# A second product of 512 tokens instead of 288, with the 64 tokens left of each batch as a ninth block

## The chip, the cores and the metric

The kernel runs on one core of a Trainium2 chip. The metric is the device time of one execution in microseconds (us). The core's engines work side by side, each through its own instructions in order: TensorE (PE in the profile; PEld is its weight load), VectorE (DVE), ScalarE (ACT), GpSimd (POOL) and SyncE (SP), which here issues the DMAs.

## The reference, cut to what matters

```python
def _attn_ref(q, k, v):                 # 8 batches, 8 heads, 576 tokens, 64 wide
    ...
    return (A @ Z @ C @ v)              # Z: six Newton steps on a 32x32 matrix

def _moe_ref(x, w_in, w_out):           # x: 4608 x 512, w_in: 512 x 2048, w_out: 2048 x 512
    h = x @ w_in
    g = np.where(h > 0.0, h, np.exp(np.minimum(h, 0.0)) - 1.0)
    return g @ w_out

def _moe2_ref(x, w1, w2, w3, w_out):    # w1..w3: 512 x 768, w_out: 768 x 512
    h = np.maximum(np.maximum(x @ w1, x @ w2), x @ w3)
    return h @ w_out
```

The 4608 tokens are 8 batches of 576. The change lies in `g @ w_out` of the middle function, called the second product here, and in what stands around it.

## The kernel before, in words

**Two phases.** The first phase makes, batch by batch, the attention, `h`, `g` and the second product, and leaves its result, called xs, in HBM. The second phase (lines 1321 and 1405) makes the last function from xs in blocks of 768 and 512 tokens by a scheme with seven products in place of eight.

**Products in three parts.** Each float32 operand is held as two tensors, a rounded high part and the rest (`wo` hi and lo, `gt[:, 0]` and `gt[:, 1]`, `ah` and `al`, `wp[:, 0]` and `wp[:, 1]`), and each product is three matmuls: high by high, low by high, high by low.

**Slots.** The first phase has 256 slots, each one (batch, half, f): half is one of two halves of 288 tokens, f one of 16 chunks of 128 of the 2048 columns of `h`. `h_mm` (line 859) issues 6 matmuls of 288 columns into one of two PSUM banks; the two factors are W' (`wp`, the attention's small matrix times w_in, four chunks of four f each, made by `w_step`, lines 812 to 843) and the attention's other factor (`ah`, `al`, one pair per half). ScalarE then makes relu and exp (lines 863, 864), VectorE joins them (871). In the next slot ScalarE casts the result into a tile `gt` (880), and GpSimd, in batch 0 in half of the slots VectorE, makes its low part (886). `gt` has LAG = 3 buffers of 288 tokens. `x_mm` (line 906) follows three slots later: for each of four blocks `ec` of 128 output columns three matmuls of 288 columns, 12 in all, into one of four PSUM banks, summed over the 16 f of a half. After the last f the four banks are copied out (lines 930 to 934) and stored to xs (935). 

**The order of the work** is the list `seq`. Batches 1 to 7 take half 0 with all f, then half 1 with all f. Batch 0, in which the weights w_in and w_out are still being converted from 64-bit words, takes half 0 with f 0 to 7, half 1 with the same, then both with f 8 to 15: its partial sums are stored, loaded again (922) and added (930).

**What rides along.** The attention of the next batch is done in steps at fixed slots (`STEP_SLOTS`, `SECOND_SLOTS`). Its matmuls (line 262) go into two PSUM banks; a step that finds its bank unread waits. The W' chunks of batch b are made at slots -6, -4, -2 and 1 counted from the batch's first slot (`W_SLOTS`), each into its own tile, and serve both halves. `w_step` needs both banks: ScalarE copies them (826), then VectorE subtracts (831). A second list converts the last function's weights (`Narrowing`), in slots 15 to 30 of most batches.

**Queues.** PE and VectorE run in the order in which the program issues; ScalarE up to slot 27 and SP up to slot 14. After that the order on ScalarE and SP is made by a scheduler when the kernel is built. A DMA that waits on SP holds up those behind it.

**The end of the first phase.** In batch 7 `background()` makes the first weights of the second phase (`weights2`), in slots 3 and 10 to 29, and from slot 28 `tk.prepare()` and `tk.make()` make the first block's operands; three slots of `x_mm` are left after the loop.

Of the kernel before, what the change touches and what calls it, by code (L numbers as in the profile page):

```python
# [19 lines left out]
def landmark_attention_mlp_maxout_kernel(  # L20
# [31 lines left out]
    LAG = 3  # L52

    FIXED_SP, FIXED_ACT = 14, 27
    RA = 3
# [27 lines left out]
    G_LOW = [[1, 0] * 8, [1, 0] * 8]  # L83
# [12 lines left out]
    hs = tc.dram_tile([NT // 512, P, 7, NP, 256], F32, name="hs")  # L96

# [412 lines left out]
    def exp_t(b, g):  # L510
        e = state.pop(("e", b, g))
        if b == 0:
            if g:
                em = r_s.tile([P, CH - 1, P], F32, tag="gt", name="et", bufs=LAG)
            else:
                em = att.tile([P, CH, P], F32, tag="et", name="et")[:, : CH - 1]
                state["tails"] = r_s.tile([P, 2, P], F32, tag="gt", name="et", bufs=LAG)
# [299 lines left out]
    def w_step(b, n, late=False):  # L817
# [27 lines left out]
    xos = {}  # L845
# [30 lines left out]
    def gt_cast():  # L876

        for key, e in held:
            gts[key] = gt = r_s.tile([P, 2, HF], F32R, tag="gt", name="gt", bufs=LAG)
            state["cast"] = nc.scalar.copy(gt[:, 0], e)  # L880

    def gt_low():
        for (b, half, f), e in held:
            gt = gts[b, half, f]
            eng = nc.vector if b == 0 and G_LOW[half][f] else nc.gpsimd
            state["low"] = eng.tensor_tensor(  # L886
                out=gt[:, 1], in0=e, in1=gt[:, 0].bitcast(F32), op=ALU.subtract
            )
        held.clear()

    def x_mm(b, half, f):
        gt = gts.pop((b, half, f))

        parts = b == 0
        first = f % (KF // 2) == 0 if parts else f == 0
        last = f % (KF // 2) == KF // 2 - 1 if parts else f == KF - 1
        if b == 0:
            assert conv.ready >= index["out", f]
        if first:
            for ec in range(KD):  # L900
                xacc[ec] = ps_x.tile([P, 512], F32, tag=f"x{ec}", name=f"x{ec}")

        for ec in (0, 2, 1, 3):
            wh, wl = [w[:, ec * P : (ec + 1) * P] for w in w_out_tiles(f)]
            for j, (a, c) in enumerate(((wh, 0), (wl, 0), (wh, 1))):
                nc.tensor.matmul(  # L906
                    xacc[ec][:, :HF],
                    a,
                    gt[:, c],
                    start=(first and j == 0),  # L910
                    stop=(last and j == 2),
                )
        t0 = b * S + half * HF
        there = [
            xs[eh * 2 * P : (eh + 1) * 2 * P, t0 : t0 + HF].rearrange("(e p) t -> p e t", p=P)
            for eh in range(2)
        ]
        add = parts and f >= KF // 2
        if first and add:
            for eh in range(2):  # L920
                xos[eh] = r_s.tile([P, 2, HF], F32, tag=f"xo{eh}", name="xo")
                nc.sync.dma_start(out=xos[eh], in_=there[eh])
        if last:
            for eh in range(2):
                if not add:
                    xos[eh] = r_s.tile([P, 2, HF], F32, tag=f"xo{eh}", name="xo")
                for ec in range(2):
                    o, a = xos[eh][:, ec], xacc[2 * eh + ec][:, :HF]
                    if add:
                        nc.vector.tensor_tensor(out=o, in0=a, in1=o, op=ALU.add)  # L930
                    elif ec == 0:
                        nc.scalar.copy(o, a)  # L932
                    else:
                        nc.vector.tensor_copy(o, a)  # L934
                nc.sync.dma_start(out=there[eh], in_=xos[eh])

# [340 lines left out]
    def tokens(nb):  # L1277
# [19 lines left out]
        def spare(nm):  # L1297
            if nb == 0:
                tag = {"S1": "wo20", "S2": "wo21", "S4": "wo30"}[nm]
                return r_w.tile([P, 2, TH], F32, tag=tag, name="s")  # L1300
# [98 lines left out]
    def o_mm(nb, tk, j, then):  # L1399
# [12 lines left out]
        there = out[ub * TB : (ub + 1) * TB].rearrange("(h r p) e -> r p h e", h=2, p=P)[r]  # L1412
        if nb < NBO - 1 or j == 0:
            nc.sync.dma_start(out=there, in_=ob.rearrange("p (h e) c -> p h (e c)", h=2))
        else:
            for n in (0, 3, 1, 2):
                c0 = n % 2 * (DM // 2)
                nc.sync.dma_start(out=there[:, n // 2, c0 : c0 + DM // 2], in_=ob[:, n])
# [60 lines left out]
    W_SLOTS = [-6, -4, -2, 1]  # L1479
    SECOND_W = [-5, -3, -1, 2]  # L1480
# [8 lines left out]
    places += [("wp", n, g) for n in range(NCH // 2, NCH) for g in range(2)]  # L1489
# [140 lines left out]
    seq = [(0, half, p * KF // 2 + f) for p in range(2) for half in range(2) for f in range(KF // 2)]  # L1630
    seq += [(b, half, f) for b in range(1, B) for half in range(2) for f in range(KF)]
# [28 lines left out]
    for n in range(1, NCH):  # L1660
        tw = (0, FPN, KF, KF + FPN)[n]
        at(tw - (2, 3, 2)[n - 1], w_both, n)
# [3 lines left out]
    for it in range(2 * NP):  # L1666
        for n, (nw, t0) in enumerate(((Narrowing(*plain[it]), 15), (Narrowing(*split7[it]), 23))):
# [5 lines left out]
            if n:  # L1673
                parts = nw.parts()
                for m in range(7):
                    behind[t0 + 11 + m].append(parts)
# [4 lines left out]
    def stage(fn, k, *args):  # L1681
        if FRONT <= k < len(items):
            fn(k, *args)

    for t, sl in enumerate(seq):
# [12 lines left out]
        if t >= LAG:  # L1698
            x_mm(*seq[t - LAG])
# [16 lines left out]
        if i == 2:  # L1716
# [5 lines left out]
        if i > KF + LAG and (i - KF - LAG) % 2:  # L1722
# [136 lines left out]
```

## Time and profile before

| | |
|---|---|
| Time, median of 3 runs | 1300.81 us (1300.03 to 1300.85) |
| Span of the profiled execution, first to last instruction | 1298.6 us |
| Median less span | 2.2 us |
| PE busy in the span | 98% |
| Batch 0 begins; batches 1 to 7 begin | 35.2; 138.4, 231.3, 322.0, 412.7, 503.4, 594.1, 684.8 us |
| Second phase begins | 762.5 us |

The profile comes from one execution; its span leaves out what lies before the first and after the last instruction, so the times of the runs stand a little above it. Matmuls overlap: the time of one in the profile is longer than the distance from its start to the next one's. What a stream of them costs is read from the time at which each begins, or from the chain, which counts that distance.

### The profile page before, as it was taken

The numbers are of one execution on the slowest core, as the hardware profiler recorded it, in microseconds if no ns is written. First come the engines' busy times: TensorE is split into PE (matmuls) and PEld (weight loads), VectorE is DVE, ScalarE is ACT, GpSimd is POOL, SyncE is SP. The second block draws the span as 40 slices with busy tenths as digits, with TensorE's granted clock in tenths as the row PEclk, the third lists the DMA queues.
The fourth block names the chain that finished last, engine by engine and source line by source line (L and its number), as shares of the span: only waits on it lengthen the run. The fifth ranks groups of instructions, "written<-read, shape, count | busy, mean of one in ns | idle before, by whom it ended". The sixth has DMA issues, their size and how long they took to land.

```text
span 1298.6 us, 26490 instructions
## 1 busy us (share of the span) xinstructions
PE 1276.0 (98%) x10196; PEld 1206.8 (93%) x10196; DVE 819.6 (63%) x1498; ACT 681.7 (52%) x1551; POOL 644.8 (50%) x609
## 2 busy tenths in 40 slices
PE   6899999999999999999999999999999999999998
PEld 3688899998998998999999999999999999999998
DVE  7888547456465475375453558776766666569773
ACT  5887557657667577576576643323131323245551
POOL 2426225435445345354256566756565656555542
PEclk8999999999999999999999999999999999999999
DMA  7944033142152143143142135555555556969852
GB/s 275 367 162 137 20 101 118 68 140 79 68 174 92 54 141 108 44 143 105 52 137 86 52 125 172 170 170 167 166 170 170 177 172 208 336 197 355 297 165 82
DMA packets 113967, 195.45 MB, mean 151 GB/s; under 512 B 7216, under 2 KB 61744, under 8 KB 113840
## 3 DMA queue, kind: packets, MB, share of 16 engines
q1 hardware_dynamic: 113840, 193.75, 45.0%
q8 instruction: 80, 1.31, 0.4%
q14 instruction: 47, 0.39, 0.1%
HBM read 134.74 MB, written 58.98 MB: 149 GB/s over the span
## 4 chain that ended last, share of the span: by engine, by line
PE 93%; ACT 2%; DVE 2%; DMA 2%; issue 1%; SPq 0%; POOL 0%; DVEq 0%; ACTq 0%
PE p L1321 31%; PE x L906 30%; PE ph L859 14%; PE p L1405 10%; PE bank L262 7%; DMA words<-in_moe_w_in_dram 2%; PE idle L262 0%; DVE eh L871 0%; ACT eh L864 0%; DVE wf L149 0%; ACT xo L1095 0%; ACT eh L863 0%; ACT words L132 0%; ACT wp L826 0%; DVE kT L323 0%
## 5 line engine op out<-in xcount | busy, mean ns | idle before, releaser
L906 PE MATMUL x<-gt,wo 128*128 128x288 f32 x3072 | 460.7, 298 | 2.2 <-ACT xo L932 1.6
L906 PEld LDWEIGHTS x<-gt,wo 128*128 128x128 f32 x3072 | 416.1, 188 | 43.2 <-ACT eh L863 18.2
L886 POOL TENSOR_TENSOR gt<-eh,gt 128x288 fp32r<-128x288 f32 x240 | 198.3, 828 | 332.1 <-ACT gt L880 326.8
L1321 PE MATMUL p<-xo,w 128*128 128x384 f32 x1944 | 349.8, 337 | 0.8 <-DVE xo L934 0.8
L1321 PEld LDWEIGHTS p<-xo,w 128*128 128x128 f32 x1944 | 341.6, 188 | 1.1 <-ACT s L1148 1.1
L859 PE MATMUL ph<-ah,wp 128*128 128x288 f32 x1024 | 244.9, 295 | 4.8 <-DVE eh L871 4.8
L871 DVE SCALAR_TENSOR_TENSOR eh<-eh,ph 128x288 f32<-128x288 f32 x256 | 113.9, 445 | 163.9 <-ACT eh L864 140.4
L1165 POOL TENSOR_TENSOR u<-s,v 128x768 f32<-128x768 f32 (+1 forms) x72 | 131.0, 1820 | 161.0 <-DVE v L1163 161.0
L859 PEld LDWEIGHTS ph<-ah,wp 128*128 128x128 f32 x1024 | 177.9, 188 | 6.8 <-DVE eh L871 6.6
L880 ACT CAST gt<-eh 128x288 fp32r<-128x288 f32 x256 | 110.0, 430 | 118.5 <-PE x L906 81.6
L1148 ACT COPY s<-p 128x384 f32<-128x384 f32 (+1 forms) x110 | 52.5, 478 | 217.5 <-PE p L1321 203.4
L863 ACT ACTIVATE eh<-ph 128x288 f32<-128x288 f32 x256 | 104.9, 410 | 94.3 <-PE ph L859 92.6
L859 PE MATMUL ph<-al,wp 128*128 128x288 f32 x512 | 150.8, 294 | 0.0
L1405 PE MATMUL p<-wo,ho 128*128 128x256 f32 x1134 | 134.3, 281 | 0.0
L1405 PEld LDWEIGHTS p<-wo,ho 128*128 128x128 f32 x1134 | 134.3, 189 | 0.0
L864 ACT ACTIVATE eh<-eh 128x288 f32<-128x288 f32 x256 | 113.8, 444 | 6.7
L1180 DVE TENSOR_TENSOR t<-p,u 128x384 f32<-128x384 f32 x108 | 56.9, 553 | 65.1 <-POOL u L1165 61.7
L859 PEld LDWEIGHTS ph<-al,wp 128*128 128x128 f32 x512 | 96.1, 188 | 0.2 <-issue 0.2
L1395 DVE TENSOR_TENSOR ho<-hf,ho 128x768 fp32r<-128x768 f32 x54 | 73.5, 1391 | 12.6 <-ACT ho L1393 12.6
L1393 ACT CAST ho<-hf 128x768 fp32r<-128x768 f32 x63 | 50.5, 836 | 45.4 <-PE p L1405 22.3
L1163 DVE TENSOR_TENSOR v<-p,s 128x384 f32<-128x384 f32 (+1 forms) x72 | 37.3, 518 | 52.5 <-PE p L1321 40.7
L1321 PE MATMUL p<-w,w 128*128 128x384 f32 x324 | 65.2, 335 | 0.0
(186 smaller groups left out, 1484.2 us busy)
## 6 DMA issues: line engine op xcount, KB each, us to landing
w<-wus SPq DMA_DIRECT2D x54, 512.0 KB, 4.2
hf<-hs SPq DMA_DIRECT2D x63, 384.0 KB, 4.9
xs<-xo SPq DMA_DIRECT2D x36, 288.0 KB, 2.9
qT<-in_q_dram SPq DMA_DIRECT2D x16, 576.0 KB, 6.1
kT<-in_k_dram SPq DMA_DIRECT2D x16, 576.0 KB, 7.4
words<-in_moe_w_dram SPq DMA_DIRECT2D x9, 1024.0 KB, 5.4
xf<-xs SPq DMA_DIRECT2D x12, 768.0 KB, 5.1
hs<-t SPq DMA_DIRECT2D x18, 512.0 KB, 3.5
```

The source lines that it names most:

```text
L262: ins = fn(*args, **kw)
L859: nc.tensor.matmul(ph[:, :HF], a, c, start=(g == 0 and j == 0), stop=(g == 1 and j == 2))
L863: nc.scalar.activation(e, ph[:, :HF], AF.Relu, scale=-1.0)
L864: state["exp"] = nc.scalar.activation(e, e, AF.Exp, scale=-1.0)
L871: state["post"] = nc.vector.scalar_tensor_tensor(out=e, in0=e, scalar=1.0, in1=ph[:, :HF], op0=ALU.subtract, op1=ALU.max)
L880: state["cast"] = nc.scalar.copy(gt[:, 0], e)
L886: state["low"] = eng.tensor_tensor(out=gt[:, 1], in0=e, in1=gt[:, 0].bitcast(F32), op=ALU.subtract)
L906: nc.tensor.matmul(xacc[ec][:, :HF], a, gt[:, c], start=(first and j == 0), stop=(last and j == 2),)
L1165: nc.gpsimd.tensor_tensor(out=u57, in0=s57, in1=v.unsqueeze(1).to_broadcast([P, 2, width]), op=ALU.add)
L1321: nc.tensor.matmul(dst, l, r, start=(c == 0 and j == 0), stop=(c == 1 and j == 2))
L1395: eng.tensor_tensor(out=lo, in0=v, in1=hi.bitcast(F32), op=ALU.subtract)
L1405: nc.tensor.matmul(dst, l, r, start=(c == 0 and n == 0), stop=(c == NP - 1 and n == 2))
```

## The change

**Second product.** `gt` holds both halves of one f (576 tokens, GT = 3 buffers). `seq` takes, in every batch, f by f with the two halves in turn. `x_mm` takes tokens 0 to 511 of a batch at once, in two parts of 6 matmuls of 512 columns, one part per slot, four slots behind (LAG = 4). Batch 0 has no partial sums any more. The result is copied out per `ec` into tiles of the tag "wq".

**The 64 left.** When the low part of a second half is made, SP stores tokens 512 to 575 of that `gt`, high and low, to a new HBM tensor `gs` (128 stores of 64 KB, in runs of 256 bytes). After batch 7 a ninth block runs the second product on them: 8 batches by 64 tokens are again 512. `load_rest` fetches 512 KB for each f into the `gt` buffer that the f three places before has left.

**Order of xs.** xs now holds the 512 of each batch first, then the ninth block. The output's stores in the second phase go to the rows to which each tile of 128 tokens belongs: two stores per tile pair in place of one, and two of 64 rows each for tiles of the ninth block.

**W' in three places.** With the halves in turn each chunk serves 8 slots running, so three pairs of tiles do (WP), made at slots -5, 1, 6 and 11 (batch 1: -4, 1, 6, 11; batch 0: at slots 4, 13, 18). `ah` and `al` have four buffers instead of three.

**The end.** The first weights of the second phase are made in every other slot of batch 7 from slot 14, and in the ninth block, where the first block's operands are made too.

```diff
-    LAG = 3
+    LAG = 4
+    GT = 3
+    XN = 512
+    REST = S - XN
+    WP = 3
...
-    RA = 3
+    RA = 4
...
-    EARLY = {2: range(8, 21), 3: range(8, 26)}
+    EARLY = {1: range(0, 11), 2: range(8, 20)}
...
-    PAIRS = "i0 i0 o0 i1 i1 o2 o4 o6 i2 i2 o8 i3 i3 o10 o12 o14".split()
+    PAIRS = "i0 i0 o0 i1 i1 o2 o4 i2 i2 o6 o8 i3 i3 o10 o12 o14".split()
...
+    gs = tc.dram_tile([KF, P, 2, B * REST], F32, name="gs")
...
-            wt = r_wp.tile([P, 2, 512], F32R, tag=f"wp{n}{g}", name="wp")
+            wt = r_wp.tile([P, 2, 512], F32R, tag=f"wp{(b * NCH + n) % WP}{g}", name="wp")
...
     def gt_low():
         for (b, half, f), e in held:
...
+            if half:
+                nc.sync.dma_start(
+                    out=gs[f, :, :, b * REST : (b + 1) * REST],
+                    in_=gt[:, :, XN:].bitcast(F32),
+                )
...
+    def load_rest(f):
+        gts[B, f] = t = r_s.tile([P, 2, S], F32R, tag="gt", name="gt", bufs=GT)
+        nc.sync.dma_start(out=t[:, :, :XN].bitcast(F32), in_=gs[f])
+
+    def x_mm(b, f, part):
+        gt = gts[b, f]
...
+        for ec in (2 * part, 2 * part + 1):
+            if f == 0:
+                xacc[ec] = ps_x.tile([P, XN], F32, tag=f"x{ec}", name=f"x{ec}")
             wh, wl = [w[:, ec * P : (ec + 1) * P] for w in w_out_tiles(f)]
             for j, (a, c) in enumerate(((wh, 0), (wl, 0), (wh, 1))):
                 nc.tensor.matmul(
-                    xacc[ec][:, :HF],
+                    xacc[ec],
                     a,
-                    gt[:, c],
+                    gt[:, c, :XN],
...
+            if f == KF - 1:
+                xo = r_s.tile([P, XN], F32, tag="wq", name="xo", bufs=4)
+                if ec % 2 == 0:
+                    nc.scalar.copy(xo, xacc[ec])
+                else:
+                    nc.vector.tensor_copy(xo, xacc[ec])
+                nc.sync.dma_start(
+                    out=xs[ec * P : (ec + 1) * P, b * XN : (b + 1) * XN], in_=xo
+                )
...
-    W_SLOTS = [-6, -4, -2, 1]
-    SECOND_W = [-5, -3, -1, 2]
+    W_SLOTS = [-5, 1, 6, 11]
+    SECOND_W = [-4, 1, 6, 11]
+    FIRST_W = [None, 4, 13, 18]
...
-    seq = [(0, half, p * KF // 2 + f) for p in range(2) for half in range(2) for f in range(KF // 2)]
-    seq += [(b, half, f) for b in range(1, B) for half in range(2) for f in range(KF)]
+    seq = [(b, half, f) for b in range(B) for f in range(KF) for half in range(2)]
...
+    def x_slot(t):
+        n, part = divmod(t, 2)
+        b, f = divmod(n, KF)
+        x_mm(b, f, part)
+        if part and n + GT >= B * KF and n + GT < (B + 1) * KF:
+            load_rest(n + GT - B * KF)
...
-    for t in range(LAG):
-        for _ in range((2, 1, 1)[t]):
+    for t in range(len(seq), len(seq) + NSL + LAG):
+        x_slot(t - LAG)
+        i = t - len(seq)
+        background()
+        if i % 3 == 0:
+            tk.prepare()
+        if i % 3 == 1:
             tk.make()
-        x_mm(*seq[t - LAG])
```

## Rows read from the trace of the kernel before

**Rows 1.** The page: span, and the chain by engine and by line.

```profile
span 1298.6 us, 26490 instructions
...
PE 93%; ACT 2%; DVE 2%; DMA 2%; issue 1%; SPq 0%; POOL 0%; DVEq 0%; ACTq 0%
PE p L1321 31%; PE x L906 30%; PE ph L859 14%; PE p L1405 10%; PE bank L262 7%; DMA words<-in_moe_w_in_dram 2%; PE idle L262 0%; DVE eh L871 0%; ACT eh L864 0%; DVE wf L149 0%; ACT xo L1095 0%; ACT eh L863 0%; ACT words L132 0%; ACT wp L826 0%; DVE kT L323 0%
```

**Rows 2.** The page's groups: the second product's matmuls.

```profile
L906 PE MATMUL x<-gt,wo 128*128 128x288 f32 x3072 | 460.7, 298 | 2.2 <-ACT xo L932 1.6
```

**Rows 3.** Stretches: us, busy time of each engine, granted clock, DMA share, GB/s.

```profile
35.20:85.00 49.80, 43.92 (x420) 38.28 (x419) 45.13 (x99) 43.84 (x101) 19.58 (x24) 1.00 0.79 282
85.00:138.40 53.40, 52.13 (x443) 46.28 (x442) 43.47 (x87) 38.52 (x91) 25.07 (x28) 1.00 0.38 129
412.70:503.40 90.70, 90.70 (x828) 83.56 (x828) 50.49 (x123) 58.80 (x147) 40.27 (x48) 1.00 0.30 103
...
462.00:467.00 5.00, 5.00 (x40) 5.00 (x40) 3.54 (x8) 4.29 (x12) 0.92 (x2) 1.00 0.98 315
467.00:472.00 5.00, 5.00 (x41) 5.00 (x40) 4.58 (x11) 3.55 (x9) 3.59 (x4) 1.00 0.61 223
477.00:482.00 5.00, 5.00 (x47) 4.00 (x46) 3.93 (x5) 3.37 (x10) 4.84 (x6) 1.00 0.07 27
...
684.80:762.60 77.80, 76.85 (x579) 76.31 (x578) 37.19 (x69) 53.24 (x129) 49.06 (x53) 1.00 0.22 66
```

**Rows 4.** The chain in order of time: start us, us, what.

```profile
688.12 1.59 PE x L906 x12
...
690.50 1.59 PE x L906 x12
...
764.51 396.67 PE p L1321 x2262
1161.19 134.17 PE p L1405 x1134
```

**Rows 5.** Timeline: attention steps on two widths, and a W' step's readers.

```profile
53.36 0.71 PE L262 MATMUL bank<-kT,qs 64*32 64x288 f32 x16
...
500.67 1.09 PE L262 MATMUL bank<-w_in_sb,mt 64*32 64x512 f32 x16
...
501.85 1.08 ACT L826 CAST wp<-bank 128x512 fp32r<-128x512 f32 x2
...
502.96 1.29 DVE L831 TENSOR_TENSOR wp<-bank,wp 128x512 fp32r<-128x512 f32 x2 [0.68 <-ACT wp L826]
```

**Rows 6.** What PE waited for: us in total, times, longest.

```profile
PE ph L859 <- DVE eh L871: 4.8, 4, 1.8
PE x L906 <- ACT xo L932: 1.6, 1, 1.6
...
PE p L1321 <- DVE xo L934: 0.8, 1, 0.8
...
PE x L906 <- DVE xo L930: 0.4, 1, 0.4
```

**Rows 7.** Timeline: a Newton step's operand, and the matmul that reads it.

```profile
469.44 0.29 DVE L787 TENSOR_TENSOR rr<-bank,rr 128x128 f32<-128x128 f32 x1 [0.28 <-ACT rr L784]
...
469.98 0.55 PE L262 MATMUL bank<-rr,rd 128*128 128x64 f32 x4
```

**Rows 8.** DMA: the queue's packets, MB, share; issues with KB, us to landing.

```profile
q1 hardware_dynamic: 113840, 193.75, 45.0%
...
w<-wus SPq DMA_DIRECT2D x54, 512.0 KB, 4.2
...
words<-in_moe_w_in_dram SPq DMA_DIRECT2D x16, 512.0 KB, 10.2
```

**Rows 9.** Timeline, SP: one issue without a wait; the output's last four stores.

```profile
494.19 0.37 SPq L311 DMA_DIRECT2D v<-in_v_dram  x1
...
1293.73 2.44 SPq L1418 DMA_DIRECT2D out_dram<-ob  x4
```

More of the change, by code (lines that the diff above doesn't have):

```diff
@@ L906, in x_mm @@
                 nc.tensor.matmul(
-                    xacc[ec][:, :HF],
+                    xacc[ec],
                     a,
-                    gt[:, c],
-                    start=(first and j == 0),
-                    stop=(last and j == 2),
-                )
[L913 to L935, printed above, removed]
+                    gt[:, c, :XN],
+                    start=(f == 0 and j == 0),
+                    stop=(f == KF - 1 and j == 2),
+                )
+            if f == KF - 1:
[7 more added lines that the diff above has]
+                )
+        if part:
+            del gts[b, f]
     TB = 768
@@ L1411, in o_mm @@
         ub, r = divmod(nb * (OH // P) + j, TH // P)
[L1412 to L1418, printed above, removed]
+        last = nb == NBO - 1 and j == 1
+        for n in (0, 3, 1, 2) if last else (0, 2):
+            h, c0 = n // 2, n % 2 * (DM // 2)
+            src = ob[:, n] if last else ob[:, n : n + 2].rearrange("p e c -> p (e c)")
+            there = out[:, c0 : c0 + DM // 2] if last else out
+            m = 2 * (TH // P) * ub + h * (TH // P) + r
+            if m * P < B * XN:
+                r0 = m * P // XN * S + m * P % XN
+                nc.sync.dma_start(out=there[r0 : r0 + P], in_=src)
+                continue
+            for i in range(P // REST):
+                r0 = (m * P - B * XN + i * REST) // REST * S + XN
+                nc.sync.dma_start(
+                    out=there[r0 : r0 + REST], in_=src[i * REST : (i + 1) * REST]
+                )
     w_out_sb = {}
@@ L1488, in landmark_attention_mlp_maxout_kernel @@
     places = [("wo", f // 2, hl) for f in range(KF - 2, KF // 2 - 1, -2) for hl in (1, 0)]
-    places += [("wp", n, g) for n in range(NCH // 2, NCH) for g in range(2)]
+    places += [("wp", n, g) for n in EARLY for g in range(2)]
     before, planned, later = {}, {}, {}
@@ L1675, in landmark_attention_mlp_maxout_kernel @@
                 for m in range(7):
-                    behind[t0 + 11 + m].append(parts)
+                    behind[t0 + 13 + m].append(parts)
     def form(k):
@@ L1683, in stage @@
             fn(k, *args)
+    def x_slot(t):
[4 more added lines that the diff above has]
+            load_rest(n + GT - B * KF)
+        if b == B and part and f % 2:
+            m = f // 2
+            if m < RING:
+                passed.add(m)
+            if m == RING - 1:
+                free.append("w")
     for t, sl in enumerate(seq):
@@ L1715, in landmark_attention_mlp_maxout_kernel @@
         i = t - (B - 1) * NSL
-        if i == 2:
+        if i == 13:
             att.release()
```

49 lines of the change are left out of this document (15 added, 34 removed).

## The prediction

> **What bounds the kernel now.** The page's chain comes first: 93% of it is PE, and the second product, line 906, has 30% of the span [rows 1]. The groups give its count, 3072 matmuls, and no more than 2.2 us of idle time before them [rows 2]. The stretches then show where that holds. From 412.7 to 503.4 us, one whole batch, PE is busy 90.70 of 90.70 us while ACT has 58.80 and DVE 50.49: PE alone sets the pace. Only batch 0 differs: in its first 49.8 us DVE is busy 45.13 and ACT 43.84, and PE 43.92 [rows 3]. The clock is 1.00 in all of them, the 2.4 GHz level, so neither version gains or loses by it. The time can only fall by as much as PE's stream gets shorter.
>
> **The second product itself.** The arithmetic does not shrink: before, 256 slots x 12 matmuls x 288 columns; after, 9 blocks x 16 x 12 = 1728 matmuls x 512 columns, the same 884,736 columns. What can shrink is the part of a matmul that does not depend on its columns. The chain gives three widths. 288 columns: 12 take 1.59 us, 132.5 ns each. 384 columns: 396.67 us for 2262, 175.4 ns. 256 columns: 134.17 us for 1134, 118.3 ns [rows 4]. At 2.4 columns per ns they would take 120.0, 160.0 and 106.7 ns, so 12.5, 15.4 and 11.6 ns stand beside the columns. No row shows 512 columns in this form, so I bound it. If the rest is constant, 512 columns cost 132.5 + 224 / 2.4 = 225.8 ns. If it grows as it does from 288 to 384 columns (42.9 ns for 96, 0.447 a column), 132.5 + 224 x 0.447 = 232.6 ns. Between the two I go by the attention's steps, the only rows with the same work at 288 and at 512 columns: 0.71 and 1.09 us for 16 matmuls [rows 5], 0.38 us for two rounds of two passes over 224 more columns, 0.424 ns a column. That gives 132.5 + 224 x 0.424 = 227.5; I take 228.5, a little towards the wide end, since 384 columns stood above that line too. Before: 3072 x 132.5 = 407.0 us. After: 1728 x 228.5 = 394.8 us. **Term 1: -12.2 us**, with ends at -16.8 and -4.6.
>
> The Trainium skill (TensorE: Matmul & The Clock Gate, Back-to-back issue gap) gives the distance of warm matmuls as columns / 2.4 plus 2.5 ns. By it 512 columns take 215.8 ns and the term would be -34.1 us; at 288 columns it says 122.5 ns where the row says 132.5, so the sum goes by the rows.
>
> **Waits that go.** The first copy-outs inside batch 0 held PE for 1.6 and 0.4 us (ACT xo, DVE xo) [rows 6]: the next f needed the banks at once. Now a bank is wanted again one part later, and batch 0 has one copy-out instead of four. **Term 2: -2.0** (0 to -2.0). At the end of the first phase PE stands 77.80 - 76.85 = 0.95 us in batch 7 [rows 3] and 0.8 us for DVE xo [rows 6], because the first operands of the second phase, the last `gt` and the copy-outs share ACT, DVE and POOL. In the ninth block 32 parts of 6 x 228.5 ns, 43.9 us, have no `h`, and these operands have it to themselves. **Term 3: -1.75** (0 to -1.75).
>
> **Batch 0.** A slot loses 1.59 - 6 x 0.2285 = 0.22 us of PE work to the ninth block. In the first 14 slots (49.8 us) DVE is 91% and ACT 88% busy with conversions, in order, and those don't shrink: of 14 x 0.22 = 3.1 us I expect a third. **Term 4: +2** (0 to 3.1). The second product begins one slot later, so up to one part of 1.37 us that lay in this stretch is done at the end instead: **+1** (0 to 1.4). PE's waits there for DVE eh, most of the 4.8 us [rows 6], stay.
>
> **Batches 1 to 6.** The slots shrink by 0.22 us each, and everything off PE must still fit. ACT goes from 65% to some 70% of a batch, but not evenly: ACT is busy 4.29 of 5 us from 462, DVE 4.58 from 467, POOL 4.84 from 477 [rows 3], where Newton steps, softmax and conversions meet. One Newton operand is ready at 469.73 and read at 469.98 [rows 7], a quarter of a us for a slot that shortens by 0.22. A W' step at slot 11 is followed by the transposes at slot 12; from its start to DVE's last read of the banks take 3.6 us (500.67 to 504.25) [rows 5], against 1.03 + 1.37 + 0.79 = 3.2 us until the next step. Steps queued on PE behind such a wait are that slot's second product and the next `h`. I put 0.7 us a batch on all of it. **Term 5: +4** (0 to 14).
>
> **The stores of the 64 left.** 128 more issues on SP, 0.37 us each [rows 9], 47 us in 600 on a queue that is otherwise waiting: nothing, unless a `gt` buffer is held. A store waits for POOL's low part and must land before the cast of the f three further on, five slots later, more than 10 us. On the DMA engines: 45.0% of 16 x 1298.6 us over 113,840 packets is 82 ns a packet [rows 8], and 32,768 packets at that price are 168 us of all engines, a share of up to 0.29 on top of 0.22 to 0.38 [rows 3]. In batch 0's first stretch 7 stores add 9 us to a share of 0.79: just covered. Zero, its bound being rival C below.
>
> **The loads of the ninth block.** Three buffers: f + 3 is fetched when f is done and wanted two f later, 2 x 12 x 0.2285 = 5.5 us. The nearest row of that size, `w` of 512 KB, lands 4.2 us after its issue [rows 8]. The first fetch may also have to wait for batch 7's last store. **Term 6: +2** (0 to 10).
>
> **The output's end.** The last four stores take SP 2.44 us with their waits, and one issue 0.37 [rows 9]; now there are eight, and one more stands behind the last result. **Term 7: +0.4** (0 to 0.8). The moved W' chunks, the fourth `ah` and the moved conversions change no count: their cover is PE's stream, and their price where it fails is in term 5.
>
> **Sum.** -12.2 - 2.0 - 1.75 + 2 + 1 + 4 + 2 + 0.4 = -6.6 us. The profiled span is 1298.6 us and would become 1292.0; runs stand 2.2 us above the span, so 1300.8 becomes **1294**.
>
> **The rivals.**
>
> A, the forecast: 1294, its own range 1285 to 1299. Chance 0.55.
>
> B, the batches don't shrink where they are full: slots 17 to 27 of batches 1 to 6 keep their length since ACT, DVE and POOL stand at 86 to 97% there [rows 3]. 11 x 6 x 0.22 = 14.5 us instead of 4: **1304.5, slower**. For it: those three rows. Against: PE never waited in that batch. It decides once more than 13 us is lost there. Chance 0.13.
>
> C, the ninth block waits for its loads. If they land like `words`, 10.2 us for the same size on a busy queue [rows 8], each third f waits 10.2 - 5.5 us, 16 / 3 times: 25 us instead of 2, **1317**. It passes +0.2% from a landing of about 7.6 us on. Against: the DMA share at that time is 0.22 [rows 3]. Chance 0.11. The Trainium skill (DMA: Bandwidth & Descriptors, Specifications) says that pieces under 512 bytes are read, modified and written; that would raise the price of the stores of 256 bytes, and no row here shows such a piece.
>
> D, the change doesn't do what it says: a wide matmul costs more per column as from 288 to 384, 232.6 ns. Term 1 is then -5, **1301**, no change. For it: 12.5 and 15.4 ns. Chance 0.14.
>
> E, the excess of 288 columns goes almost entirely and 512 columns take 215.8 ns: 1294 - 21.9 = **1272**. Against: 256, 288 and 384 columns all stand 11 ns or more above their columns [rows 4]. Chance 0.07. This is what the skill's formula would give.
>
> **How the numbers follow.** 0.2% is 2.6 us, about what a measurement can tell: faster below 1298.2, slower above 1303.4. Faster: A 0.53, E 0.07, D's low part 0.04: 0.64. Same: A 0.01, D 0.08, B 0.05, C 0.01: 0.15. Slower: B 0.08, C 0.10, D 0.02, A 0.01: 0.21. The range, 1282 to 1306, leaves out E, the far part of C and a little of B. Its low end is term 1 at 225.8 ns with terms 2 and 3 and little lost; its high end is B, or C with 8 us.
>
> **What would show it.** In the chain after: 12 matmuls of line 906's successor in 2.74 us, 228.5 ns each (225.8 and 232.6 tell term 1's ends, 215.8 tells E). A batch like that from 412.7 takes 84 to 85 us (rival B: over 86), and PE's waits for DVE rr, DVE eh or a bank come up in it. Batch 0 takes some 96 us instead of 103.2, W' steps moved out included. The ninth block takes 44 to 46 us with no wait on a DMA (rival C: more). The second phase keeps 397 and 134 us. The prediction is wrong if the pitch stands outside 225.8 to 232.6, or if PE waits more than 12 us in what it adds.

## The result, and the profile after

The kernel with the change takes **1318.37 us**, the median of 4 runs (1317.35 to 1320.37), against 1300.83 for the kernel before: a ratio of 1.0137 [1.0122, 1.0151]. It is slower by 17.5 us, where the forecast was 6.6 us faster. The profiled execution has a span of 1318.6 us; it is the longest of the four, so the differences below add up to 20.0 us and not to 17.5.

The page of the kernel after: span, the chain by engine, the second product's matmuls (with the idle time before them), and the DMA queue, to be held against [rows 1, 2, 8].

```profile
span 1318.6 us, 24092 instructions
...
PE 87%; DVE 6%; ACT 3%; DMA 1%; issue 1%; POOL 0%; SPq 0%; DVEq 0%; ACTq 0%; POOLq 0%
...
L919 PE MATMUL x<-gt,wo 128*128 128x512 f32 x1728 | 459.2, 404 | 5.5 <-DMA gt<-gs 5.5
...
q1 hardware_dynamic: 147680, 208.18, 48.4%
```

PE has fallen from 93% to 87% of the chain, and a wait of 5.5 us for a DMA stands before the second product where 2.2 us for copy-outs stood. The 512-column matmul's mean of 404 ns says nothing about its price, as these overlap. The chain does, here in order of time in batch 7 of the kernel after (start us, us, what), against [rows 4]:

```profile
690.80 0.80 PE ph L864 x6
691.60 1.39 PE x L919 x6
692.98 0.79 PE ph L864 x6
693.78 1.40 PE x L919 x6
```

Six matmuls take 1.39 to 1.40 us, 232.3 ns each by the mean over many such parts; 228.5 was forecast.

To see where the time went, the span is cut at five places that both traces have: the first `h` matmul of batch 0, of batch 1 and of batch 7, the first matmul of the second phase, and the last matmul of all. (The table ahead of the prediction puts the starts of batches 1 to 7 two slots late. Counted by slots they are 133.67, 225.3, 316.0, 406.7, 497.4, 588.1 and 678.8 us, and batch 0 took 98.5 us, not 103.2.)

| stretch | before | after | difference | by the forecast's terms |
|---|---|---|---|---|
| start to batch 0 | 35.16 | 36.69 | +1.5 | 0 |
| batch 0 | 98.51 | 95.27 | -3.2 | -7.0 |
| batches 1 to 6 | 545.2 | 515.6 | -29.6 | -38.2 |
| batch 7 and ninth block, to the second phase | 83.67 | 132.98 | +49.3 | +38.2 |
| second phase | 532.85 | 532.09 | -0.8 | 0 |
| behind the last matmul | 3.29 | 5.94 | +2.65 | +0.4 |
| sum | 1298.6 | 1318.6 | +20.0 | -6.6 |

The fourth column is worked out from the prediction: a batch sheds 32 x 0.22 = 7.0 us; batch 0 also sheds term 2 and gives 2 us of term 4 back; term 5 is in the third line; the ninth block's 43.9 us, batch 7's 7.0, term 3, term 6 and the 1 us of term 4 are in the fourth.

The stretches of the kernel after: slots 0 to 16 of batch 0; one whole batch (the fourth, batch 3); then four pieces of the ninth block; the second phase (columns as in [rows 3]):

```profile
36.69:88.09 51.40, 42.97 (x340) 33.12 (x339) 46.80 (x99) 44.41 (x100) 20.49 (x25) 0.97 0.67 238
303.61:389.87 86.26, 85.65 (x636) 69.09 (x634) 51.13 (x121) 58.41 (x146) 40.20 (x49) 1.00 0.37 117
721.28:744.13 22.85, 21.44 (x92) 16.80 (x91) 19.99 (x25) 9.68 (x19) 13.18 (x9) 1.00 0.79 262
744.13:749.81 5.68, 1.56 (x7) 0.94 (x5) 4.30 (x5) 1.39 (x3) 2.81 (x3) 0.94 0.76 206
749.81:755.10 5.29, 5.29 (x13) 4.13 (x14) 0.00 (x0) 0.00 (x0) 0.00 (x0) 0.50 0.47 176
755.10:780.57 25.47, 25.47 (x109) 20.63 (x108) 6.37 (x9) 4.57 (x9) 3.23 (x3) 0.98 0.60 191
780.57:1312.66 532.09, 532.09 (x3403) 531.77 (x3401) 360.12 (x438) 170.07 (x299) 297.86 (x204) 1.00 0.60 197
```

And the same slots 0 to 16 in the kernel before:

```profile
35.16:86.44 51.28, 45.40 (x430) 39.76 (x429) 46.58 (x103) 44.96 (x102) 20.70 (x25) 1.00 0.78 281
```

Three things are to be seen. In slots 0 to 16 PE has 2.43 us less to do, and the stretch is no shorter: 51.28 and 51.40 us, with VectorE and ScalarE busy as before (46.58 and 46.80, 44.96 and 44.41). A full batch is still PE's: 85.65 of 86.26 us. In the ninth block PE stands for over 4 us of the piece from 744.13, and then works 5.29 us at a granted clock of 0.50, the 1.2 GHz level, in which it issues 13 matmuls; at 232.3 ns they would have taken 3.0 us.

What PE waited for in the kernel after (us in total, times, longest), against [rows 6]:

```profile
PE ph L864 <- DVE eh L876: 5.7, 6, 1.8
PE x L919 <- DMA gt<-gs: 5.5, 3, 4.1
...
PE bank L268 <- DVE wp L837: 2.9, 5, 1.3
PE bank L268 <- DVE rr L793: 2.0, 2, 1.5
PE bank L268 <- ACT et L540: 1.7, 1, 1.7
```

The waits for `xo` of terms 2 and 3 are gone. The one for the DMA is new, and SP's own instructions in the kernel after (start us, us, what) show where it comes from:

```profile
736.56 0.52 SPq L907 DMA_DIRECT2D gt<-gs  x1
743.46 0.52 SPq L1228 DMA_DIRECT2D raw<-w2s  x1
744.07 1.03 SPq L907 DMA_DIRECT2D gt<-gs  x1
```

The load issued at 736.56 has a successor that is issued only at 744.07. What stands between them on SP is a load of weights for the second phase (`raw`). The chain of the kernel after, in order of time, says what that one waits for, and PE's instructions before it say when the load could have gone:

```profile
742.98 0.42 DVE tt L958
743.40 0.02 SPq L1228
...
744.07 5.70 DMA gt<-gs
...
749.81 0.79 PE x L919
```

```profile
733.47 8.63 PE L919 MATMUL x<-gt,wo 128*128 128x512 f32 x36 [0.88 <-DMA gt<-gs]
...
742.63 3.05 PE L919 MATMUL x<-gt,wo 128*128 128x512 f32 x12 [0.53 <-DMA gt<-gs]
```

VectorE reads the last of the buffer's old weights until 743.40; then the `raw` load goes out, then the ninth block's load, which takes 5.7 us, and PE goes on at 749.81. From there ten f are left of the sixteen, so this is the load of f 6. Its buffer is that of f 3, the second of the three f that begin at 733.47, and was free at about 733.47 + 24 x 0.2323 = 739.0. The load went out some 5 us after that.

The output's last stores on SP in the kernel after, against the 2.44 us of [rows 9]:

```profile
1306.05 0.34 SPq L1411 DMA_DIRECT2D out_dram<-ob  x1
1306.48 9.69 SPq L1415 DMA_DIRECT2D out_dram<-ob  x10
```

### The profile page after: what moved, and what is told of

Read it like the earlier page. It is cut to its first block, busy times and chain, and to the rows that moved or that the text cites. A ratio compares the mean times of both kernels' runs of the same rounds, so it can differ in the third digit from the quotient of the medians.

```text
span 1318.6 us, 24092 instructions
## 1 busy us (share of the span) xinstructions
PE 1281.7 (97%) x8852; PEld 1130.0 (86%) x8852; DVE 828.3 (63%) x1476; ACT 681.5 (52%) x1537; POOL 642.6 (49%) x609
## 4 chain that ended last, share of the span: by engine, by line
PE 87%; DVE 6%; ACT 3%; DMA 1%; issue 1%; POOL 0%; SPq 0%; DVEq 0%; ACTq 0%; POOLq 0%
PE p L1312 30%; PE x L919 27%; PE ph L864 14%; PE p L1396 10%; PE bank L268 6%; DMA v<-in_v_dram 1%; DVE eh L876 1%; DVE wp L837 1%; DVE tt L958 0%; DVE w_in_sb L155 0%; ACT eh L868 0%; DMA gt<-gs 0%; ACT wp L832 0%; ACT wf L133 0%; ACT gt L887 0%
## 5 line engine op out<-in xcount | busy, mean ns | idle before, releaser
L919 PE MATMUL x<-gt,wo 128*128 128x512 f32 x1728 | 459.2, 404 | 5.5 <-DMA gt<-gs 5.5
L919 PEld LDWEIGHTS x<-gt,wo 128*128 128x128 f32 x1728 | 309.6, 190 | 101.3 <-issue 34.1
L1312 PE MATMUL p<-xo,w 128*128 128x384 f32 x1998 | 358.3, 337 | 0.0
L1312 PEld LDWEIGHTS p<-xo,w 128*128 128x128 f32 x1998 | 351.0, 188 | 0.2
L864 PE MATMUL ph<-ah,wp 128*128 128x288 f32 x1024 | 248.1, 298 | 6.2 <-DVE eh L876 5.7
L1319 DVE TENSOR_TENSOR t<-t 128x1536 f32<-128x1536 f32 x36 | 63.3, 1757 | 3.1 <-DVE t L1174 0.5
```

The lines of the kernel that those rows point to most:

```text
L864: nc.tensor.matmul(ph[:, :HF], a, c, start=(g == 0 and j == 0), stop=(g == 1 and j == 2))
L919: nc.tensor.matmul(xacc[ec], a, gt[:, c, :XN], start=(f == 0 and j == 0), stop=(f == KF - 1 and j == 2),)
L1312: nc.tensor.matmul(dst, l, r, start=(c == 0 and j == 0), stop=(c == 1 and j == 2))
```

## The experiments

None of the versions of the changed kernel below is faster than the kernel before. All ratios are to the kernel before on the same chip. "Start", "batch 0" and so on are the stretches of the table above.

### Is the price in the column, or in the matmul?

All but the first and the last of the 48 matmuls of a bank are issued as two of 256 columns, so that the columns stay and the count of matmuls nearly doubles.

```diff
+                first = f == 0 and j == 0
+                whole = first or (f == KF - 1 and j == 2)
+                step = XN if whole else XN // 2
+                for c0 in range(0, XN, step):
-                nc.tensor.matmul(xacc[ec], a, gt[:, c, :XN], start=..., stop=...)
+                    nc.tensor.matmul(xacc[ec][:, c0:c0+step], a, gt[:, c, c0:c0+step], start=first, stop=...)
```

> Edit: all but the first and the last of the 48 matmuls into a bank are done as two of 256 columns, 3312 more or less in place of 1656. Theory C (cost by columns): 256, 288, 384 and 512 columns cost 118.3, 132.4, 175.3 and 232.3 ns, one line of 0.445 ns a column and 4.3 ns a matmul. Then two halves cost 236.6 ns and the time rises by 1656 x 4.3 ns = 7 us, to 1324 to 1327. Rival W (the wide ones are dear for another reason, such as the layout of gt or the full bank): the halves are either as cheap as their columns, 2 x 106.7 + 4.3, and the time falls by some 25 us, or dearer than 118.3 ns, and it rises by over 12 us.

Measured: 1325.01 us, 1.0185 [1.017, 1.02], 6.6 us above the kernel with the change. The chain in batch 7 of this kernel:

```profile
691.83 1.43 PE x L923 x12
...
694.05 1.42 PE x L923 x12
```

Twelve halves in 1.42 to 1.43 us are 118.7 ns each, and two of them cost some 5 ns more than one whole. So doubling the count costs some 5 ns for each matmul more, and nearly all of the price is in the columns. With 118.3 ns at 256, 132.3 at 288 (a slot of 18 of them takes 2.38 us), 175.3 at 384 and 232.3 at 512 columns the four widths lie on one line, 0.445 ns a column and 4.3 ns beside it. Term 1 was to come from the part beside the columns, and that part is 4.3 ns, not 12.5: (3072 - 1728) x 4.3 = 5.8 us is all that there was to gain, and 1728 x 232.3 - 3072 x 132.3 = -5.0 is what came.

### The ninth block: the data, the queue, the clock

The first version issues the loads from ScalarE's queue instead of SP's:

```diff
-        nc.sync.dma_start(out=t[:, :, :XN].bitcast(F32), in_=gs[f])
+        nc.scalar.dma_start(out=t[:, :, :XN].bitcast(F32), in_=gs[f])
```

> Edit: the ninth block's loads from gs are issued by ScalarE instead of SP; nothing else. Theory Q (order on SP): in the changed kernel the load that PE waited 4.1 us for was issued 7 us late, because loads of the second phase's weights that wait for a buffer stood ahead of it on SP. Then the waits for gs go (under 1 us in all), the clock does not fall to its 1.2 GHz level in the ninth block, and the time falls by 8 to 10 us, to 1308 to 1311. Rival L (landing): the loads themselves land too late, 512 KB each in runs of 2 KB beside other traffic; then PE waits at about the same places and the time stays at 1315 or more.

Measured: 1314.33 us, 1.0108 [1.0091, 1.0125]: 4.0 us of the 17.5 back, about half of what was expected. PE's wait in this kernel, and the chain that leads to its end:

```profile
PE x L919 <- DMA gt<-gs: 1.9, 1, 1.9
```

```profile
722.23 1.56 POOL gt L894
...
723.81 5.03 DMA gs<-gt
...
728.94 5.10 DMA gt<-gs
...
734.09 2.19 PE x L919 x7
```

The wait falls from 5.5 to 1.9 us, but one is left, and the clock is at half for 3.4 us from 735.5 on. It is another wait than the one on SP: GpSimd's last low part of batch 7, its store (5.03 us), and only then a load that had to stand behind that store (5.10 us).

The second version has no stores to `gs` and no loads from it; the ninth block multiplies the tile that is left in the buffer sixteen times.

```diff
-            if half:
-                nc.sync.dma_start(
-                    out=gs[f, :, :, b * REST : (b + 1) * REST],
-                    in_=gt[:, :, XN:].bitcast(F32),
-                )
...
     def load_rest(f):
-        gts[B, f] = t = r_s.tile([P, 2, S], F32R, tag="gt", name="gt", bufs=GT)
-        nc.sync.dma_start(out=t[:, :, :XN].bitcast(F32), in_=gs[f])
+        if f == 0:
+            state["same"] = gts[B - 1, KF - 1]
+        gts[B, f] = state["same"]
```

> Edit: no stores to gs and no loads from it; the ninth block multiplies the last tile of batch 7 sixteen times, so the 512 tokens of that block are not the reference's. Theory Q: as the run with the loads on ScalarE, 1307 to 1311, and the batches keep their 85.6 to 86.2 us, since the 128 stores of 256-byte runs cost nothing. Rival S (stores): the stores hold gt tiles or the DMA engines; then the batches become shorter by 0.5 us or more each and the time falls to 1305 or below.

Measured: 1310.74 us, 1.0074 [1.0057, 1.0091], inside the expected range. PE never stands in the ninth block, whose 36 parts are 36 x 1.395 = 50.2 us in both kernels, and the fourth stretch takes 123.88 us instead of 132.98. The same batch as above, in this kernel:

```profile
303.61:389.87 86.26, 85.73 (x637) 69.45 (x637) 51.01 (x121) 58.63 (x148) 40.58 (x49) 1.00 0.31 107
```

It is as long as with the stores (batches 1 to 6 take 85.6 to 86.3 us in either kernel): 128 stores in runs of 256 bytes cost the batches nothing that can be measured, although the DMA share falls from 0.37 to 0.31 without them. And this is as far as repairs of the loads alone can go: with its data for nothing the ninth block still leaves the change 10.0 us slower than before. By the spans: start +2.3, batch 0 -3.5, batches 1 to 6 -29.9, the end +40.2, second phase -0.8, tail +2.5.

The third version keeps the loads on SP and issues the `raw` load of the next weight only at the fourth step of the current one, where it has its buffer sooner after the issue.

```diff
         while k < 7:
+            if k == 3 and n + 1 < AHEAD2:
+                raw2(n + 1)
...
-        if n + 1 < AHEAD2:
-            raw2(n + 1)
```

> Edit: in weights2 the loads of the next piece's raw weights are issued four steps later, when their buffer is nearly free; the ninth block's loads stay on SP. Theory Q (order on SP): nothing stands long ahead of the ninth block's loads, PE waits under 1 us for gs in all, the clock does not fall there, and the ninth block gets 7 to 9 us shorter: 1309 to 1311.5, more than the 4 us that the loads on ScalarE gave. Rival L (landing): the waits stay over 3 us and the time is 1314 or more.

Measured: 1315.38 us (1314.28 to 1318.1), 1.0118 [1.0103, 1.0133]. Its waits:

```profile
PE x L919 <- POOL gt L894: 1.4, 1, 1.4
...
PE x L919 <- DMA gt<-gs: 1.1, 1, 1.1
```

The wait for the loads falls from 5.5 to 1.1 us, so the order on SP was the cause of most of it. The clock then stays at its full level in the whole ninth block, and the fourth stretch falls to 128.29 us, by 4.7 us where 7 to 9 were expected. Part of what is missing is a new wait of 1.4 us. GpSimd's instructions in this kernel show it:

```profile
722.82 2.07 POOL L1261 TENSOR_TENSOR w<-raw,w 128x512 fp32r<-128x512 f32 x2 [2.39 <-ACT w L1259]
724.85 0.78 POOL L894 TENSOR_TENSOR gt<-eh,gt 128x288 fp32r<-128x288 f32 x1
```

The last `gt`'s low part is made behind 2.07 us of low parts of the second phase's weights.

### Why batch 0 kept its length

Three versions tried to shorten it from its ends: LAG of 3 instead of 4; the conversion of w_out earlier; and GpSimd alone making the low parts.

```diff
-    LAG = 4
+    LAG = 3
```

> Edit: LAG = 3, so the second product begins in slot 3 again; nothing else. Theory E (early stretch): with LAG = 4 PE stands so much in slots 0 to 3 that the clock falls to the 1.2 GHz level from 42.5 to 45.9 us, and one part of 1.4 us moves from a stretch in which ScalarE and VectorE set the pace to the end. With LAG = 3 the clock stays at its higher level there, slot 4 loses 1 to 2 us, one part less stands behind the loop, and the time falls by 1.5 to 3 us against the changed kernel, to 1315.5 to 1317. Rival: the stretch keeps its length, since ScalarE and VectorE set it whatever PE does, and the time falls by 1.4 us or less.

Measured: 1319.67 us, 1.0146 [1.0131, 1.0162]; batch 0 takes 95.78 us. One slot of second product more in the stretch did not shorten what follows, and the half clock of 3.4 us in slots 3 and 4 stayed where it was. The expectation missed; its rival, that the stretch keeps its length, is what came.

```diff
-    FIRST_W = [None, 4, 13, 18]
+    FIRST_W = [None, 4, 10, 18]
-    EARLY = {1: range(0, 11), 2: range(8, 20)}
+    EARLY = {1: range(0, 11), 2: range(8, 17)}
```

> Edit: batch 0's third W' chunk is made at slot 10 instead of 13 (and the words of items 17 to 19 go to other places). Theory P (ScalarE and VectorE set the first 17 slots of batch 0, 51.3 us before and 51.4 after): the waits of 1.7 and 1.3 us for a PSUM bank at slots 13 and 14 go, others come, and slots 0 to 16 still take 51 us; the time changes by less than 1 us. Rival B (the bank waits themselves are the loss): slots 0 to 16 take 48 to 49 us and the time falls by 2 to 3 us, to 1315.5 to 1316.5.

Measured: 1318.58 us, 1.0143 [1.0126, 1.016], and 51.10 us for slots 0 to 16: no change.

```diff
-    G_LOW = (1, 0)
+    G_LOW = (0, 0)
```

> Edit: in batch 0 of the changed kernel all low parts of gt are made by GpSimd, none by VectorE (16 of 32 before the edit, 0.46 us each on VectorE). Theory P (ScalarE and VectorE set the pace of batch 0's first 17 slots, so that PE's saving there is lost): with 3.7 us less for VectorE in these slots they take 1.5 to 3.5 us less than 51.4, batch 0 takes 92 to 94 us in place of 95.3, and the time falls by 1.5 to 3.5 us against 1318.4. Rival A (ScalarE alone, or the order of the steps): under 1 us. Rival G: GpSimd is late with its low parts, and the time rises.

Measured: 1317.2 us, 1.0124 [1.011, 1.0138]. Batch 0 takes 92.99 us, 2.3 less, and the half clock in slots 3 and 4 is gone; the time falls by 1.2, within the intervals of the two. Slots 0 to 16 take 50.45 us, 0.95 less, where 1.5 to 3.5 were expected; VectorE is busy 45.05 us in them instead of 46.80. VectorE's load matters there, but that it alone sets the pace is not shown. The same edit on the kernel before:

> Edit: the same on the kernel before. If VectorE sets the pace there, its first 17 slots fall from 51.3 us by 1 to 3 us, and the time to 1298 to 1300, below both kernels. If not, it stays within 1 us of 1300.7; if GpSimd is late for a second product that follows three slots later instead of four, it rises by 1 us or more.

Measured: 1300.02 us, 0.9992 [0.9983, 1.0001]: no change that can be told, so VectorE's low parts did not hold the kernel before back.

What settles the question is work added. Fourteen matmuls of 512 columns more, 14 x 232.3 ns = 3.3 us for PE, are put into f 0 to 6 once in batch 0 and once in batch 3:

```diff
+            products = ((wh, 0), (wl, 0), (wh, 1))
+            if b == 0 and f < 7 and ec % 2 == 0:
+                products = ((wh, 0), (wl, 0), (wl, 0), (wh, 1))
-            for j, (a, c) in enumerate(((wh, 0), (wl, 0), (wh, 1))):
+            for j, (a, c) in enumerate(products):
```

> Edit: in batch 0, for f 0 to 6, each part of the second product does one matmul of 512 columns twice (slots 4 to 17; the low by high product counts twice there, so batch 0's result differs). That is 14 x 232 ns = 3.25 us more for PE, about what the change took out of these slots. Theory P (ScalarE and VectorE set the pace there, PE has room): slots 0 to 16 take 51.4 to 52.4 us, and batch 0 lengthens by under 1.2 us. Rival (PE sets the pace, the bank waits are separate losses): batch 0 lengthens by 3 us or more.

> Edit: the same 14 matmuls more, but in batch 3, where PE has no room. Both theories: batch 3 (86.25 us in the changed kernel's profile) lengthens by 3.25 us, 3.0 to 3.4, less the waits of up to 0.9 us that it already has.

Measured, one execution of each: 1318.09 us with the work in batch 0, 1321.32 with it in batch 3. The stretch of batch 0 in the first, and that of batch 3 in the second:

```profile
36.67:132.46 95.79, 87.14 (x627) 68.92 (x626) 81.58 (x169) 76.59 (x177) 42.57 (x50) 0.98 0.55 188
```

```profile
303.43:392.43 89.00, 88.72 (x650) 71.83 (x649) 50.57 (x121) 58.46 (x146) 40.06 (x49) 1.00 0.35 114
```

The same 3.3 us lengthen batch 0 by 0.52 us (95.27 to 95.79) and batch 3 by 2.75 (86.25 to 89.00, where a wait of 0.48 us for `wp` took in the rest). In batch 0 PE has room, and what is taken away there gains next to nothing; in batch 3 PE is the bound. The chain of the kernel after agrees. In slots 0 to 16 it has no instruction of PE at all (in the kernel before it had 9.2 us of them), only ScalarE and VectorE by turns, as here (start us, us, what):

```profile
44.91 0.44 ACT eh L869
45.35 0.33 ACT gt L887
...
45.71 0.46 DVE gt L894
46.17 0.36 DVE eh L876
46.53 1.03 DVE wf L155
```

In batch 3, 81.5 of its 86.26 us are PE's. Which of ScalarE and VectorE would have to get faster in batch 0, or whether both, these runs don't show.

### The output's stores

The output is written in the order of the tiles, one store for 128 rows, with no rows split in two:

```diff
-            if m * P < B * XN:
-                r0 = m * P // XN * S + m * P % XN
-                nc.sync.dma_start(out=there[r0 : r0 + P], in_=src)
-                continue
-            for i in range(P // REST):
-                ...
+            nc.sync.dma_start(out=there[m * P : (m + 1) * P], in_=src)
```

> Edit: the output is written in the order of the tiles, one store per 128 rows, so the rows of the result stand in another order than the reference's. Theory T: of the 5.9 us from the last matmul's end to the end of the span (3.3 us before), 2.3 to 2.7 us come from the last tile's eight stores of 64 rows; the tail becomes 3.3 to 3.6 us and the time 1315.5 to 1316.5. Rival: the tail is the landing of earlier stores and stays over 5 us.

Measured: 1316.5 us, 1.012 [1.0105, 1.0135]; behind the last matmul 3.71 us instead of 5.94. The last stores on SP:

```profile
1304.16 7.66 SPq L1409 DMA_DIRECT2D out_dram<-ob  x6
```

Four of these six issues are the last tile's; the kernel with the change has eight for it among its ten. The stores by halves of 64 rows are the tail's 2.2 us.

### Repairs together

LAG of 3, the late `raw` load, and another order of the last phase's blocks, so that the ninth block's rows don't come last:

```diff
+    ORD = (0, 1, 2, 3, 4, 5, 7, 8, 6)
```

> Edit: LAG = 3, the later raw loads, and the last phase's blocks in the order 0 to 5, 7, 8, 6, so that the last tile is none of the ninth block's and is written by four stores of 128 rows. If the three losses are separate (early stretch 1.5 to 3 us, ninth block 7 to 9, tail 2.2 to 2.6) they add up to 11 to 14 us: 1304 to 1307, still above the kernel before, because the wide matmuls give only some 5 us and batch 0 gives nothing. If it falls below 1301, the losses that I put down to batch 0 and to the columns are smaller than I think.

Measured: 1315.64 us, 1.0116 [1.0101, 1.0131]. The tail is 3.52 us as wanted, but with LAG 3 PE waits for `gt` from ScalarE (0.97 us) and GpSimd (1.57) where the ninth block begins, the clock falls to half for 6.8 us from 728.1, and batch 0 takes 96.97.

The loads on ScalarE's queue with the late `raw` load, the order of blocks and GpSimd's low parts, all with LAG 4:

> Edit: on the changed kernel, the ninth block's loads on ScalarE, the later raw loads, the last phase's blocks in the order 0 to 5, 7, 8, 6, and batch 0's low parts on GpSimd. From the single edits: 7 to 9 us for the ninth block, 2.2 for the tail, up to 3 for batch 0; 1305 to 1309. The kernel before (1300.7) is then still ahead: what is left is a part of 6 x 232.3 ns per f for a start in which ScalarE and VectorE hide it. Below 1301 I would be wrong about that.

Measured: 1314.38 us, 1.0102 [1.0088, 1.0116]. The tail is 3.30 us and batch 0 93.72, but the waits for the loads are back (0.72, 1.79 and 0.73 us). ScalarE's instructions and its queue in this kernel:

```profile
737.86 0.53 ACTq L907 DMA_DIRECT2D gt<-gs  x1
...
743.31 0.40 ACT L1259 CAST w<-tt 128x256 fp32r<-128x256 f32 x1 [4.78 <-DVE tt L958]
743.37 0.53 ACTq L907 DMA_DIRECT2D gt<-gs  x1
```

Between two loads lie 5.5 us, in which ScalarE stands with a cast of the second phase's weights that waits 4.78 us for VectorE: what held SP now holds ScalarE. Both versions missed. In these two the gains of single edits did not add: each edit moved what the next one leans on.

### The later start

Batch 0 begins at 36.5 to 37.5 us in every version of the kernel after. To see whether 35.16 was one execution's chance, the kernel before again; and the kernel after with fewer of the first words loaded into the tiles of the second W' chunk:

> The kernel before, unchanged, for a second profile. If the later start of batch 0 (36.5 to 37.5 us in the changed kernel's profiles, 35.2 before) belongs to the change, this profile shows 35.2 within 0.4 us; if it is the spread of executions, it shows up to 37.

> Edit: the places of W' chunk 1 take words only from item 8 on, instead of from item 0. If the two loads of words that the changed kernel issues some 10 us earlier at the start are why batch 0 begins 1.3 to 2.9 us later, it begins at 34.6 to 35.6 us again and the time falls by 1.5 to 2.5 us. If not, it stays at 36.5 to 37.5.

```diff
-    EARLY = {1: range(0, 11), 2: range(8, 20)}
+    EARLY = {1: range(8, 11), 2: range(8, 20)}
```

Measured: 34.64 us for the kernel before (1299.69 us in all) and 36.73 for the other (1318.27). With 35.58 in the run with its low parts on GpSimd the kernel before starts batch 0 at 34.6 to 35.6 us, so the later start belongs to the change, and those loads are not its cause. What is, stays open.

## Why the prediction was wrong

**Term 1, the second product itself: mis-sized, and it carried the sum.** It said 228.5 ns and -12.2 us; it measured 232.3 ns and -5.0, which is rival D's number. The working had the answer in its own rows: the three widths of the same kind of matmul, 118.3, 132.5 and 175.4 ns, lie on one line [rows 4], and that line gives 232.5 at 512 columns. I took the slope of the attention's steps instead [rows 5], which are other matmuls (64 rows of contraction), because they reached to 512 columns. And the excess over 2.4 columns per ns was taken for a part that does not depend on columns; it was mostly a part that does. Splitting the matmuls showed it. This is 7.2 of the 26.6 us between forecast and account, and alone it takes the forecast from faster to about no change.

**Terms 2 and 4, batch 0: the step that failed is that a wait removed shortens the stretch.** Term 2's waits did go (slots 10 to 12 shrank by 2.2 us; the 0.4 us for DVE xo lay in batch 1). They came back as other waits at slots 13 and 14 (+2.7 us), seen here in PE's instructions of the kernel after (the wait and its releaser in brackets):

```profile
74.73 1.09 PE L268 MATMUL bank<-w_in_sb,mt 64*32 64x512 f32 x16 [1.73 <-ACT et L540]
...
79.47 0.90 PE L268 MATMUL bank<-v,et 128*32 128x64 f32 x40 [1.26 <-DVE wp L837]
```

In this stretch the chain runs through VectorE and ScalarE, and PE waits wherever the order next puts it behind them. I had allowed a third of the columns' saving to survive in 49.8 us that I called 14 slots and that hold 16 and a half; of it and of term 2 nothing did, in slots 0 to 16. Nor did "neither version gains or loses by the clock" hold: PE, with less to do in the first slots, ran at half clock in slots 3 and 4, and slot 4 is 1.8 us longer. The stretch of the kernel after:

```profile
42.50:45.90 3.40, 3.28 (x12) 2.92 (x12) 2.68 (x6) 3.19 (x8) 1.33 (x1) 0.51 1.02 367
```

Batch 0 became 3.2 us shorter, all behind slot 16, but 2.4 us of that are not the columns': of the W' steps for batch 1 three lay in it before (slots 27, 29 and 31) and one does now (slot 28), and a step costs 1.21 us (a slot takes 3.40 us with one, 2.19 without). These two steps lie in batch 7 now. Of the batch's 6.2 us of columns only 0.8 came. The runs with work added show the room (0.52 us for 3.3). Missed by 5.4 us.

**Term 5, batches 1 to 6: right in kind, too small.** The batches take 85.6 to 86.3 us; 84 to 85 was forecast with the cheaper column. With 232.3 ns they should have shrunk by 6 x 6.2 = 37.2 us and did by 29.6, so 7.6 us were lost and not 4. The W' step at slot 11, as named, holds the next attention step for 0.48 us in batches 1, 3 and 5. The Newton operand of [rows 7] holds its slots too: slots 21 and 22 of batches 2 to 6 keep their 2.82 us (2.84 and 2.85 in batch 4), where most slots lose 0.19. PE's waits in these batches come to 1.8 us; the rest of the 7.6 does not show as idle time of PE, and where it lies is not settled. Rival B (slots 17 to 27 keep their length) came in these two slots alone: W' steps left out, the eleven became 1.6 us shorter in each batch.

**Term 6, the ninth block's loads: the wait came, and most of it by another way.** The term gave 2 us for loads that land too late. While weights are fetched beside them they land in about 5.7 us, where I had taken 4.2 from [rows 8], against 5.5 that were to hide them; with issues that go out some tenths late this makes the two short waits, 0.88 and 0.53 us. Rival C, with 10.2, was not what happened. The other 4.1 us come from a step that the prediction left out: it did not look at what stands ahead of a load on SP, although a DMA that waits there holds up those behind it. A `raw` load that waits for VectorE held the queue, and the load behind it went out some 5 us late. The late `raw` load brings the waits from 5.5 to 1.1 us; what the loads on ScalarE's queue leave is the wait behind batch 7's last store, which the term did name. Second, the wait has a price behind it: the clock fell to the 1.2 GHz level and the next 13 matmuls took 2.3 us more, 2.8 us in all over the 6.1 us that it lasted. The fourth stretch is 10.9 us above its columns (44.6 - 6.2 = 38.4), where the terms allowed 1.25: 5.5 of waiting, 2.8 of clock, 0.8 for the one slot of lag (4 x 1.39 - 3 x 1.59), 2.4 for the two W' steps that came from batch 0, less 1.0 for term 3's wait in batch 7. That leaves 0.4.

**Term 3 was right.** The 0.95 us that PE stood in batch 7 are gone, and so is the wait of 0.8 us for `xo`, which lay at the head of the second phase: this phase takes 532.09 us instead of 532.85.

**Term 7, the output's end: 2.65 us for 0.4.** It counted eight issues for the last tile, which is right, and put one of them behind the last result at 0.37 us. Five stand there, some 0.6 us apart:

```profile
1313.14 3.03 SPq L1415 DMA_DIRECT2D out_dram<-ob  x5
```

Rows in tile order take 2.2 us off.

**The start** (1.5 us) is in no term. **The stores of the 64 left** were costed at nothing, and the version without them agrees.

Summed, with the two W' steps booked to batch 0: term 1 7.2, batch 0 5.4, term 5 3.6, the end 6.5 (9.7 less these 2.4, and less the second phase's 0.8, which is term 3's), the tail 2.3 and the start 1.5 are 26.5 us. The range ended at 1306, since each bad case was priced alone; the time came out of three of them at once: D's columns, a part of C's wait, and costs in batches 0 to 6.

## What to carry to other kernels

Where several widths of one kind of matmul stand in a profile, put a line through them before anything is said of a cost that does not depend on the width: here it is 4.3 ns, and making 3072 matmuls into 1728 gains 5 us of 1300 for a ninth block's traffic and order. Ask of each stretch which engine ends it before work is taken off another: 3.3 us of PE's work more cost 0.5 us in batch 0 and 2.75 in batch 3, and 2.4 us less in batch 0's first half gained nothing. When steps move, ask also which stretch they move to, or a stretch looks shorter that only has less in it. When a load is added to a queue that issues in order, go through what stands ahead of it and what that waits for; and price a long wait of PE with the slow clock behind it.

## What the runs showed of the hardware

- **A column costs 0.445 ns at a granted clock of 1.00**, not 1 / 2.4 = 0.417, in the products of this kernel with 128 rows of contraction: 256, 288, 384 and 512 columns take 118.3, 132.3, 175.3 and 232.3 ns from start to start, a line with 4.3 ns beside it. Why a column costs more than a cycle stays open. The Trainium skill (TensorE: Matmul & The Clock Gate, Back-to-back issue gap) has a formula, there for an isolated matmul, that would put 512 columns at 215.8 ns; the measurement decides.
- **A wait on PE can cost more than its length.** After 4.1 us without its data PE ran at a granted clock of 0.50 for 6.1 us of its work, in which each matmul of 512 columns takes 427 ns instead of 232.3. The price varies: in the version with fewer of the first words loaded early, which has the same loads and the same wait of 4.1 us, the low stretch lasted 3.4 us, and batch 7 with the ninth block took 130.95 us instead of 132.98. The length of a wait alone does not tell: single waits of 1.1 and 1.4 us (late `raw` load) and one of 1.79 us (loads on ScalarE's queue with three more edits) show no such stretch, one of 1.9 us (loads on ScalarE's queue) shows one of 3.4 us, and waits of 0.97 and 1.57 us close together (LAG of 3) show one of 6.8 us.
- **Small pieces to HBM beside other work cost nothing here.** 128 stores of 64 KB in runs of 256 bytes, with a DMA share of 0.37 in a full batch, left the batches as long as without them.
- **A DMA that waited on SP held the one behind it.** A load of weights that waited for VectorE until 743.40 us kept a load behind it whose buffer had been free since about 739.0 until 744.07.
